# One pair of 1 MB input loads cut into rows and columns, in a gated recurrence with a slot mixture behind it

## The chip, the cores and the metric

The kernel runs on one core of a Trainium2 chip. The metric is the device time of one execution in microseconds (us), as the median of several runs; before the change it is 196.58 us (three runs, 196.49 to 196.69).

## What is computed

Two layers in a row. The first is a gated linear recurrence over 5056 tokens, for 4 batches and 256 channels; the second treats all 20224 tokens as one set and mixes them through 8 experts with 4 slots each.

```
# x, f_logit: (4, 5056, 256); lower_bound: (256,)
f = lower_bound + (1 - lower_bound) * sigmoid(f_logit)
for t in range(S):
    h = f[:, t] * h + (1 - f[:, t]) * x[:, t];  y[:, t] = h
# y as (20224, 256); phi: (256, 32); w1: (8, 256, 1024); w2: (8, 1024, 256)
logits = y @ phi
d = softmax of logits over the tokens;  slot_input = d.T @ y        # 32 slots
slot_out[e] = relu(slot_input[e] @ w1[e]) @ w2[e]                    # 8 experts, 4 slots each
c = softmax of logits over the slots;   out = c @ slot_out
```

The slots need all tokens, so the kernel has two parts with the experts between them: first everything is read, scanned and summed into slots; then the experts run on the 32 slots; then the 20 MB of output are computed and stored.

## The kernel before, in words

**Units.** The tokens of a batch are cut into 10 groups of 512 (the ninth has 448 new ones, the last is laid from the end). A unit is one group of one batch; there are `n_unit` = 40 of them, numbered from 0. Each unit passes through stages on different engines: its `f_logit` and `x` are loaded (`load`), ScalarE takes the sigmoid (`gate`, L235), GpSimd forms the product with `x` (`enter`, L246), TensorE turns both to channels (L250, L258, L265), ScalarE forms the decays (L298, L305), VectorE scans (L320, L333), TensorE turns the result back to tokens (L346) and sums it into the slots. The order of all instructions is written out by hand: one loop over the units, in which the engines get the steps of different units.

**Loads.** All inputs are loaded by SyncE in `load(n)`, called for every second unit, six units ahead of the scan (`AHEAD = 6`), `f_logit` first and `x` behind it. I write f(n) and x(n) for the two. Each fills one tile of two units, `f_t` or `x_t`; there are three buffers of each, so f(30) goes where f(24) was and can't start before the sigmoid of that tile is done, and x(30) where x(24) was, which GpSimd must have read. For units 0 to 3 and for the last four, each unit has loads of its own of 512 KB (L225). For units 4 to 31 (`long(n)`) a load is one DMA of 1 MB (L215): 1024 consecutive tokens, eight to a partition, so that each of the 128 partitions gets one run of 8 KB. Units 32 to 35, of the ninth group, use another split of 896 KB (L219). f(30) and x(30), called in unit 24, are the last pair of the long form; f(32), x(32), f(34), x(34) and the 512 KB loads of units 36 to 39 follow.

**Weights.** `w1` and `w2` (16 MB in 32-bit floats, 16 transfers of one expert's half, the last in two parts) are loaded by GpSimd (L137, L147), which writes them as 16-bit floats: four of them between the inputs, the others from unit 31 on, behind the inputs. The last two go into a tile of `f_t` (in the profile: `w_t`).

**Behind the loop.** The experts run as matmuls with `w1` (L653) and `w2` (L689, L703); `so_ps` is their sum, L715 scales it to `slot_out`, and from it the outputs are computed (L734, L813 and the scalings) and stored by SyncE in pieces of up to 4 MB.

**Names.** `P` = 128 partitions, `B` = 4 batches, `R` = 4 tokens per partition and unit, `D` = 256 channels, `G` = 512.

Of the kernel before, what the change touches and what calls it, by code (L numbers as in the profile page):

```python
# [18 lines left out]
def kernel(  # L19
# [10 lines left out]
    nc = tc.nc  # L30
    B, S, D = x.shape
# [4 lines left out]
    P = 128  # L36
    DC = D // P
    FC = F // P
    R = 4
    G = P * R  # L40
    n_grp = (S + G - 1) // G
    n_unit = n_grp * B
# [3 lines left out]
    def first(g):  # L46
        return g * G if g < n_grp - 1 else S - G

    def used(g):
        return first(g + 1) - first(g) if g < n_grp - 1 else G  # L50
# [116 lines left out]
    with tc.tile_pool(name="sp2", bufs=3) as sp2, \  # L167
# [23 lines left out]
        def long(n):  # L191
            return B <= n and by_pairs(n)

        def place(n):
            if by_pairs(n):
                t, j = divmod(n, 2 * B)
                return 2 * t + j % 2, j // 2
            return divmod(n, B)
# [4 lines left out]
        def tokens(src, n, k):  # L203
            g, b = place(n)
            v = src[ds(b, k), ds(first(g), G)]
            return v.rearrange("b (p r) d -> p b r d", r=R)

        def load(n, k=2):
            for src, dst, tag in ((f_logit, fs, "f_t"), (x, xs, "x_t")):
                if n % 2 == 0:  # L210
                    dst[n // 2] = ld.tile([P, 2, R, D], F32, name=tag, tag=tag)
                t = dst[n // 2]
                if long(n):
                    g, b = place(n)
                    nc.sync.dma_start(  # L215
                        out=t.rearrange("p u r d -> p (u r) d"),
                        in_=src[b, ds(first(g), 2 * G)].rearrange("(p r) d -> p r d", r=2 * R))
                elif n // B == odd:
                    nc.sync.dma_start(  # L219
                        out=t.rearrange("p u r d -> p (u r d)")[:, ds(0, R7 * D)],  # L220
                        in_=src[ds(n % B, 2), ds(first(odd), used(odd))].rearrange(
                            "b (p r) d -> p b (r d)", r=R7))
                else:
                    for m in range(n, n + k):
                        nc.sync.dma_start(out=t[:, ds(m % 2, 1)], in_=tokens(src, m, 1))  # L225
# [256 lines left out]
        for n in range(SINGLE):  # L482
            load(n, 1)
        load(SINGLE)
        lb_constants()
        gate(0, 1)
# [13 lines left out]
        for n in range(n_unit):  # L500
            if n < SINGLE - 2:
# [10 lines left out]
                if n % 2 == 0:  # L512
                    unit(load, n + AHEAD)
# [6 lines left out]
            else:  # L520
# [55 lines left out]
                elif not end and by_pairs(n - 1):  # L576
                    if n % B == 0:
                        g = (n - 1) // (2 * B) * 2
# [50 lines left out]
    with tc.tile_pool(name="ew", bufs=1) as ew, \  # L629
# [34 lines left out]
        for q in range(E // Q):  # L664
# [4 lines left out]
            if q == 0:  # L669
                nc.tensor.matmul(cs_ps, rep2, cs1, start=True, stop=True)  # L670
                src = ht_ps.rearrange("p f (j s) -> p f j s", s=NS)[:, :, :, ds(0, SPE)]
                src = bass.AP(tensor=src.tensor, offset=src.offset,
                              ap=[list(src.ap[0]), [P, FC], [NS + SPE, Q], [1, SPE]])
# [6 lines left out]
            for j in range(Q):  # L680
                s0 = (Q + j) * SPE
                src = ht_ps[:, :, ds(j * NS + s0, SPE)]
# [202 lines left out]
```

## Time and profile before

| | |
|---|---|
| median of three runs | 196.58 us (196.49 to 196.69) |
| the profiled execution | 196.66 us |
| its span, first to last instruction | 194.9 us |
| busy: TensorE, VectorE, ScalarE, GpSimd | 148.1, 141.8, 138.7, 102.5 us |
| read from HBM, written to it | 58.23 MB, 20.71 MB |
| SyncE's queue, share of the 16 DMA engines' span | 76.5% |
| GpSimd's queue | 21.6% |
| f(n) and x(n) of 1 MB, issue to landing, median | 12.2 and 11.0 us |

The page of the profile shows one execution. Its slices cut the span into 40 equal parts and give each engine's busy share in tenths; DMA is the mean share of the 16 DMA engines, GB/s what arrived (a weight counts half, as it is written in 16 bits). In a table by stretches, each engine has its busy microseconds and its instruction count, then come the granted clock of TensorE, the DMA share (it can pass 1, as packets of two queues overlap) and GB/s. The chain that ended last is given as start, length and what ran. A list of issues gives start, length, engine, line and tile; SPq is the queue of SyncE. A line of waits gives who waited for whom, the microseconds in total, how often, and the longest. A load that is issued waits in its queue behind others, so its 11 to 12 us to landing are mostly waiting.

### The profile page before, as it was taken

How to read it: one execution, taken by the hardware profiler on the slowest of the kernel's cores; microseconds unless marked ns; L12 is line 12 of the kernel's file. 1: busy time of each engine (PE TensorE's matmuls, PEld its weight loads, DVE VectorE, ACT ScalarE, POOL GpSimd, SP SyncE). 2: the span in 40 equal slices, each digit the busy share in tenths (PEclk: the TensorE clock that was granted, in tenths of full speed). 3: DMA queues.
4: the chain of work that ended last, by engine and by line, in shares of the span. 5: the costliest groups of instructions: out<-in, count | busy, mean ns of one | idle time of the engine just before them, and what ended most of it. 6: DMA issues, size and time to landing. Idle time of an engine off the chain costs nothing.

```text
span 194.9 us, 3264 instructions
## 1 busy us (share of the span) xinstructions
PE 148.1 (76%) x1215; PEld 106.6 (55%) x1216; DVE 141.8 (73%) x175; ACT 138.7 (71%) x193; POOL 102.5 (53%) x77
## 2 busy tenths in 40 slices
PE   0685887997999979899798976999695999970000
PEld 0464666685776757767585865667462763420000
DVE  2666799899799999999999999543178858860000
ACT  3686898799889999899988698531068789990000
POOL 2586778864998689874979978570030000000000
PEclk9998799699999999999999999999999555555555
DMA  6999999999999999999999999999839999999995
GB/s 203 415 431 427 427 429 425 425 422 375 363 425 429 406 330 427 420 432 350 380 416 410 255 219 213 215 214 213 168 142 432 424 454 431 431 431 430 431 431 222
DMA packets 11953, 70.75 MB, mean 363 GB/s; under 512 B 1297, under 2 KB 1682, under 8 KB 7458
## 3 DMA queue, kind: packets, MB, share of 16 engines
q1 hardware_dynamic: 9456, 62.13, 76.5%
q0 software_dynamic: 2480, 8.42, 21.6%
q8 instruction: 9, 0.15, 0.3%
q14 instruction: 6, 0.05, 0.1%
q10 hardware_dynamic: 2, 0.00, 0.0%
HBM read 58.23 MB, written 20.71 MB: 405 GB/s over the span
## 4 chain that ended last, share of the span: by engine, by line
PE 27%; DVE 23%; DMA 22%; ACT 12%; issue 3%; POOL 2%; SPq 1%; ACTq 0%; DVEq 0%; POOLq 0%
DVE h L333 14%; DMA w_t<-in_moe_w_dram 10%; PE op L813 7%; PE sp L250 5%; DMA w_sb<-in_moe_w_dram 5%; PE hp L346 5%; PE up L265 4%; DVE ht L365 4%; DMA f_t<-in_f_logit_dram 4%; DMA out_dram<-ob 3%; DVE h L320 3%; ACT s_t L235 3%; ACT oc L780 2%; ACT a L298 2%; POOL u_t L246 2%
## 5 line engine op out<-in xcount | busy, mean ns | idle before, releaser
L246 POOL TENSOR_TENSOR u_t<-s_t,x_t 128x1024 bf16<-128x1024 bf16 (+1 forms) x39 | 82.3, 2127 | 22.3 <-ACT s_t L235 14.0
L333 DVE TENSOR_TENSOR_SCAN h<-a,h,up 128x512 bf16<-128x512 f32 x64 | 78.1, 1268 | 6.6 <-PE up L265 2.7
L235 ACT ACTIVATE s_t<-f_t 128x2048 bf16<-128x2048 f32 (+2 forms) x23 | 38.2, 1668 | 5.1 <-DMA f_t<-in_f_logit_dram 5.0
L346 PE MATMUL hp<-ident_f,h 128*128 128x128 f32 (+1 forms) x160 | 29.1, 306 | 8.1 <-DVE ht L365 5.9
L346 PEld LDWEIGHTS hp<-ident_f,h 128*128 128x128 f32 (+1 forms) x160 | 23.4, 207 | 17.1 <-DVE ht L365 10.6
L298 ACT ACTIVATE a<-sp,lbs 128x1024 f32<-128x1024 bf16 x28 | 29.7, 1113 | 2.8 <-PE sp L250 2.7
L250 PE MATMUL sp<-ident_f,s_t 128*128 128x128 f32 x144 | 22.1, 299 | 7.3 <-ACT s_t L235 5.9
L265 PE MATMUL up<-ident_f,u_t 64*128 64x64 f32 x224 | 21.2, 233 | 2.4 <-POOL u_t L246 2.2
L250 PEld LDWEIGHTS sp<-ident_f,s_t 128*128 128x128 f32 x144 | 18.0, 154 | 9.1 <-ACT s_t L235 6.9
L728 ACT ACTIVATE ob<-op,rrow 128x256 f32<-128x256 f32 x32 | 12.3, 481 | 11.8 <-PE op L734 10.8
L265 PEld LDWEIGHTS up<-ident_f,u_t 64*128 64x128 f32 x224 | 16.7, 141 | 7.1 <-POOL u_t L246 2.9
L365 ACT COPY ht<-hp 128x512 f32<-128x512 f32 (+1 forms) x21 | 12.2, 581 | 5.3 <-PE hp L346 5.2
L305 ACT ACTIVATE a<-sp,lbs 128x512 f32<-128x512 bf16 (+2 forms) x16 | 13.2, 868 | 2.9 <-PE sp L250 2.6
L184 PE MATMUL slot_ps<-rep,ident_f 128*128 128x256 f32 x42 | 14.3, 431 | 0.0
L365 DVE COPY ht<-hp 128x512 f32<-128x512 f32 (+1 forms) x19 | 12.7, 669 | 0.9 <-PE hp L346 0.9
L813 PE MATMUL op<-slot_bd,etall 64*128 64x512 bf16 x32 | 13.1, 625 | 0.1
L824 ACT ACTIVATE oc<-op,rrow 128x256 f32<-128x256 f32 x32 | 12.2, 486 | 0.7 <-PE op L813 0.2
L734 PE MATMUL op<-slot_out,etall 32*128 32x256 bf16 x64 | 12.1, 363 | 0.1
L818 DVE TENSOR_TENSOR oc<-op,rrow 128x1024 f32<-128x1024 f32 x8 | 9.7, 1223 | 2.7 <-PE op L813 2.7
L724 DVE TENSOR_TENSOR ob<-op,rrow 128x1024 f32<-128x1024 f32 (+2 forms) x12 | 9.7, 862 | 2.6 <-DMA out_dram<-ob 2.0
L734 PEld LDWEIGHTS <-etall 32*128 32x128 bf16 x64 | 8.6, 152 | 3.6 <-issue 1.1
L379 PE MATMUL lg<-h,phi 128*32 128x512 bf16 (+1 forms) x80 | 10.5, 405 | 0.2 <-ACT et L403 0.2
(109 smaller groups left out, 166.9 us busy)
## 6 DMA issues: line engine op xcount, KB each, us to landing
f_t<-in_f_logit_dram SPq DMA_DIRECT2D x14, 1024.0 KB, 12.2
x_t<-in_x_dram SPq DMA_DIRECT2D x14, 1024.0 KB, 11.0
w_sb<-in_moe_w_dram POOLq DMA_DIRECT2D x14, 512.0 KB, 10.3
out_dram<-ob SPq DMA_DIRECT2D x3, 2048.0 KB, 10.5
f_t<-in_f_logit_dram SPq DMA_DIRECT2D x8, 512.0 KB, 8.6
x_t<-in_x_dram SPq DMA_DIRECT2D x8, 512.0 KB, 7.7
out_dram<-oc SPq DMA_DIRECT2D x1, 4096.0 KB, 14.6
out_dram<-oc SPq DMA_DIRECT2D x2, 2048.0 KB, 15.9
```

The source lines that it names most:

```text
L184: nc.tensor.matmul(slot_bank[:, 1], ident_f, wide_rep, start=first, stop=False, skip_group_check=True)
L235: nc.scalar.activation(s_t, f_t, ACT.Sigmoid, scale=-1.0)
L246: nc.gpsimd.tensor_tensor(uts[n][:, :r], s_t[:, :r], x_t[:, :r], ALU.mult)
L250: nc.tensor.transpose(ps[:, :, r], t[:, r].bitcast(F32), ident_f)
L265: nc.tensor.transpose(v[:, :, r], t(r)[k].bitcast(F32), ident_f[k, k])
L298: nc.scalar.activation(a, sp[:, :, :, :, o], ACT.Identity, scale=nomlb[:, ds(o, 1)], bias=1.0)
L305: nc.scalar.activation(decays[n // 2, o][:, ds(n % 2, k), :T], sp[:, ds(n % 2, k), :T, o], ACT.Identity, scale=nomlb[:, ds(o, 1)], bias=1.0)
L333: nc.vector.tensor_tensor_scan(h[:, :T, o], decays[n // 2, o][:, n % 2, :T], up[:, :T, o], hs[number(g - 1, b)][:, ds(used(g - 1) - 1, 1), ...
L346: nc.tensor.transpose(hp[:n_p, r], hw[:, :n_p, r], ident_f)
L365: copy(hts[g][:n_p, b].rearrange("p r d -> p (r d)").bitcast(F32), hps.pop(n)[:n_p].rearrange("p r c -> p (r c)"))
L734: nc.tensor.matmul(op[:, j], ew[:, :, r + j], slot_out[ds(b * NS, NS)], start=True, stop=True, skip_group_check=True)
L813: nc.tensor.matmul(op[:, i_r].rearrange("p u d -> p (u d)"), ew[:, :, r + i_r], slot_bd[ds(j * 2 * NS, 2 * NS)].rearrange("s u d -> s (u d)"),
```

## The change

`load` gets a list of parts for the long form. For every long load the tile and the source are now addressed with eight tokens of a partition as one run; with a single part (all 128 rows, all columns) this is one DMA as before. For unit `LEAN` = 40 - 8 - 2 = 30, x(30) becomes three DMAs: 112 rows, 8 rows, 8 rows. f(30) becomes seven: 112 rows, 8 rows, 8 rows without their last 1 KB, and that last 1 KB of these eight rows in DMAs of 4, 2, 1 and 1 rows. The bytes are the same, and so is the place where each goes; SyncE issues eight DMAs more.

```
+        LEAN = n_unit - 2 * B - 2
+        ALL = 2 * R * D
+        LEAN_F = ((0, 112, 0, ALL), (112, 8, 0, ALL), (120, 8, 0, ALL - D),
+                  (120, 4, ALL - D, D), (124, 2, ALL - D, D),
+                  (126, 1, ALL - D, D), (127, 1, ALL - D, D))
+        LEAN_X = ((0, 112, 0, ALL), (112, 8, 0, ALL), (120, 8, 0, ALL))
...
                 if long(n):
                     g, b = place(n)
-                    nc.sync.dma_start(
-                        out=t.rearrange("p u r d -> p (u r) d"),
-                        in_=src[b, ds(first(g), 2 * G)].rearrange("(p r) d -> p r d", r=2 * R))
+                    to = t.rearrange("p u r d -> p (u r d)")
+                    at = src[b, ds(first(g), 2 * G)].rearrange("(p r) d -> p (r d)", r=2 * R)
+                    parts = ((0, P, 0, 2 * R * D),)
+                    if n == LEAN and tag == "f_t":
+                        parts = LEAN_F
+                    if n == LEAN and tag == "x_t":
+                        parts = LEAN_X
+                    for p, k_p, c, k_c in parts:
+                        nc.sync.dma_start(out=to[ds(p, k_p), ds(c, k_c)],
+                                          in_=at[ds(p, k_p), ds(c, k_c)])
```

## The prediction

> **What bounds the kernel now.** I read the page's slices first, then the engines by stretches of time, the chain that ended last, SyncE's issues and the waits.
>
> ```profile
> DMA  6999999999999999999999999999839999999995
> ```
> ```profile
> 84.00:88.00 4.00, 3.82 (x30) 2.58 (x27) 4.00 (x4) 3.95 (x6) 3.98 (x3) 1.00 1.02 429
> 120.00:130.00 10.00, 9.80 (x159) 7.18 (x160) 5.28 (x9) 5.26 (x11) 7.15 (x9) 1.00 1.06 214
> 130.00:139.00 9.00, 7.61 (x102) 5.80 (x95) 3.46 (x9) 1.40 (x4) 0.51 (x2) 1.00 1.06 212
> 139.00:142.00 3.00, 2.11 (x16) 1.64 (x17) 0.01 (x1) 0.00 (x0) 0.00 (x0) 1.00 0.52 92
> ```
> Next to last is the DMA share. All 16 DMA engines work without a gap from 3 to 139 us, through the inputs and the weights behind them; only from 139 to 142 us do some run out before others.
>
> ```profile
> 111.56 10.21 DMA w_sb<-in_moe_w_dram
> 121.77 0.28 issue
> 122.06 18.78 DMA w_t<-in_moe_w_dram
> 140.83 0.04 issue
> 140.87 1.09 PE so_ps L703 x8
> 141.96 0.02 issue
> 141.99 0.50 DVE slot_out L715
> ```
> The chain ends its first part on the last weights; everything later (stores until 194 us) starts from them. So a microsecond on the DMA engine that finishes last at 141.5 us is a microsecond of the kernel, and work on an engine that finishes early is free. The DMA engines differ. The completion marks of a transfer's sixteen shares, as offsets from the first, are in the trace:
>
> ```
> x(30), first mark 86.64: 0 .02 .03 .09 .10 .13 .20 .21 .33 .52 .54 .83 1.53 1.60 1.61 1.65
> last w, first mark 139.77: 0 .09 .10 .30 .54 .55 .64 1.13 1.17 1.38 1.55 1.63 1.66 1.68 1.71 1.75
> ```
> Every engine moves 8 KB in 0.309 us (packets 0.306 apart), so the lag comes from elsewhere: instruction packets of 16 KB at 29.6, 47.3, 62.5, 77.0, 92.6, 105.0, 124.0 and 134.9 us. Each puts another engine some 1.24 us back (before 29.6 the largest offset is 0.42, after it one stands at 1.66); the 8 KB ones (44.8, 57.4, 64.8, 100.0, 135.3) cost about 0.5. The first packets of the kernel start in two groups of eight, 1.74 to 1.82 and 2.00 to 2.11 us. Following packets end to start, the first two hits fall in the second group. By the offsets that vanish at each hit I put the first seven there and the eighth (134.9) and the 8 KB ones in the first group. At the end, then, six of the second group stand at 1.55 to 1.75, and the first group at 0 to 0.64 with two at about 1.15 and 1.38.
>
> **The change part by part.** It concerns f(30) and x(30).
>
> ```profile
> 73.36 0.33 SPq L215 DMA_DIRECT2D x_t<-in_x_dram  x1
> 73.78 0.38 SPq L215 DMA_DIRECT2D f_t<-in_f_logit_dram  x1
> 78.00 0.33 SPq L215 DMA_DIRECT2D x_t<-in_x_dram  x1
> 78.42 0.66 SPq L219 DMA_DIRECT2D f_t<-in_f_logit_dram  x1
> 82.93 0.56 SPq L219 DMA_DIRECT2D x_t<-in_x_dram  x1
> 83.58 0.56 SPq L219 DMA_DIRECT2D f_t<-in_f_logit_dram  x1
> 88.78 0.54 SPq L219 DMA_DIRECT2D x_t<-in_x_dram  x1
> ```
> They are x(28), f(30), x(30), f(32), x(32), f(34), x(34).
>
> The other long loads only get another view. Their trace rows already are 128 runs of 8,192 bytes, so I cost that at nothing; were it not merged, rows of 1 KB (46 ns each) would add an eighth to every load.
>
> Bytes: each engine's share of 8 rows becomes 7; 16 rows per tensor move into narrow DMAs. The one narrow DMA of the trace, the single row of the lower bound, has its packet at 1.61 to 1.81 us, and a first-group engine starts its first row at 1.814; so I put the narrow ones on the first group. The second group then saves 2 x 0.306 = 0.61 us. The first adds 4 pieces less 2 rows: +0.57 us (the 7 KB piece at 0.27), and on one engine four 1 KB packets at 0.043 and six more completions, +0.8. In the opposite case, all on the second group, its six late engines go up by 0.6.
> The Trainium skill (DMA: Bandwidth & Descriptors, section "Why a DMA increments its semaphore by 16 and not by 1") says that a DMA from SyncE uses the largest count up to 16 that divides its rows, on the lowest-numbered engines. By that rule 112 rows use all sixteen and 8 rows the first eight, and the sum stays at the +0.57 and -0.61 above; no run here shows an 8-row load yet.
>
> SyncE: eight more issues at 0.33 to 0.5, 2.6 to 4 us. Those of f fit into the gap of 73.78 to 78.00. But SyncE's DMAs take eight semaphores in turn, and a DMA waits until the one eight before it has landed: x(4) issued at 5.66 us, x(0) landed at 5.64. GpSimd's weights do the same:
>
> ```profile
> POOL w_t L147 <- DMA w_sb<-in_moe_w_dram: 2.8, 2, 2.0
> ```
> Now eight before is eight before in ten small ones. The fifth, sixth and seventh f pieces wait for f(26), x(26), f(28) (76.0, 78.5, 80.9). The 112 rows of x wait for x(28), landed at 83.38, instead of going at 78.00. The next piece of x waits for the 112 rows of f, which the late engines finish one row sooner than the 85.86 of now: 85.55. The last x piece follows at 85.97, f(32) at 86.36 instead of 78.42, with x(32) and f(34) queued behind it; the first packet comes 1.0 us after an issue (0.72 to 1.74 at the start): 87.4. x(32) at 87.1 and f(34) at 87.7 are early enough, x(34) keeps 88.78, and from there the queue is as deep as before.
>
> What starves: x(28) ends on the early engines at 81.62; f(30) with its pieces runs to 84.4, x(30)'s first packet comes at 84.4: nothing lost. The 112 rows end at 86.5; the next pieces come at 86.55 and 86.95, to 87.2; f(32) at 87.4 to 87.6. Now f(32) starts on the early engines at 86.5, on unhit ones of the second group at 86.6 to 86.8, on the four late ones at 88.1. So the first group shifts by +0.9 (0.6 work, the rest idle), the unhit second group by +0.8 (all idle), the late four by -0.5. The start of f(32) lines all engines up, and hits after it fall on engines that have lost their lead.
>
> Sum at the last weights: second-group engines hit at 92.6 and 105.0: 1.6 + 0.8 = 2.4. First-group engine hit at 134.9: 1.38 + 0.9 = 2.3. The late four: 1.7 - 0.5 = 1.2. The largest goes from 1.75 to 2.4, **+0.6 us**, all of it on the path. Compute hides nothing and loses nothing: x(30) lands by 87.7 (88.29 now), f(32) by about 90 (91.09 now). Bounds: a first packet 0.85 us after the issue (143.60 to 144.45, a store) makes it +0.45; 1.3 us, as for a second issue of 0.66 in the way, +0.9. The profiled execution took 196.66 us, its span 194.9 and 1.8 around it; the median, 196.58, is 0.08 below. 196.58 + 0.6 = 197.2 us, own range 196.9 to 197.6.
>
> **Rivals.** No stall: if the framework lets the pieces pass without those waits, only bytes move. The second group falls to 1.14, the first rises to 1.38 + 0.7 = 2.1: +0.3, 196.9 us. Against it stand the two waits above.
>
> Faster: the rows leave the late engines as the diff arranges it, no wait bites, and the instruction packets of 134.9 and 135.3 us fall on engines that were made lighter (they follow the instruction streams, whose timing can move). Then the first group's largest is 0.84 + 0.65 = 1.5 and the second's 1.14 plus little: 1.75 to about 1.4, 196.2 us. It decides only if both conditions hold; for it speaks that six of the eight relieved engines are the latest ones.
>
> Narrow rows collide: the eight rows of a piece lie in neighbouring partitions, and if four of them must pass one at a time, a piece takes 4 x 0.309 instead of 0.309. Four pieces add 3.6 us to the first group: 1.38 + 0.6 + 3.6 = 5.6, +3.9, 200.5 us; two at a time, +1.2 on it and about 198.1. Nothing in the trace writes so few partitions from several engines; the loads at L219, split in other shapes, run at full rate (7 KB in 0.272), which speaks weakly against it.
> The Trainium skill (SBUF — State Buffer, section "Door 1: The DMA port swizzle") says that bandwidth depends on how many of 16 ports the partitions reach, four neighbours sharing one; by it rows 112 to 119 have two ports, which is the one-at-a-time case.
>
> That the change does nothing would need no landing to matter; the saturated DMA rules it out, short of terms that cancel.
>
> **How the numbers follow.** Forecast 0.45, no stall 0.15, collision 0.25, faster 0.15. 0.2%, about what a measurement of this kernel can tell from no change, is 0.39 us. Slower by more: 0.38 of the forecast, the collision, 0.05 of the second, 0.68. Within: 0.07, 0.10 and 0.05, 0.22. Faster: 0.10. The range reaches from 196.2 to 200.0, leaving out the top of the collision and the best of the faster case.
>
> **What would show it.** Right: the 112 rows of x issued near 83.4, the next x piece near 85.5 and f(32) near 86.4; a DMA share below 1 between 84 and 88; the last weights landing near 142.1. Wrong: issues of x at 78 (no stall); row packets of 0.6 us or more in the narrow pieces (collision); the last landing before 141.4 (faster).

## The result, and the profile after

The changed kernel takes 203.99 us (203.75 to 204.53, four runs); the one before took 196.6 us on the same chip. The ratio is 1.038 [1.037, 1.039]: 7.4 us slower, where +0.6 was forecast and 200.0 was the top of the range. Some executions of a kernel take one to two per cent longer than the rest (205.35 us beside 201.98 to 203.39 in one kernel below); ratios leave them out. The profiled execution took 204.19 us, its span 202.4.

The DMA share of the 40 slices, and the rates under it:

```profile
DMA  4999999999999999999999999999909999999995
GB/s 203 418 430 424 431 423 429 424 427 318 423 427 423 351 390 427 257 253 259 425 417 415 280 206 215 189 211 213 173 6 405 425 433 440 418 431 447 418 431 246
```

In the DMA row there is no dip where one was forecast, between 84 and 88 us: it reads 9 throughout. The rate below it does fall: three slices of 5 us, from 81 to 96 us, move 257, 253 and 259 GB/s where their neighbours move 425 to 427. The engines are busy, but slow. The same in steps of 2 us, for the kernel after and then for the kernel before (busy time and count of PE, PEld, DVE, ACT, POOL; then granted clock, DMA share, GB/s):

```profile
82.00:84.00 2.00, 2.00 (x22) 1.49 (x22) 2.00 (x3) 2.00 (x3) 1.01 (x1) 1.00 1.11 258
84.00:86.00 2.00, 2.00 (x19) 1.38 (x14) 2.00 (x3) 1.98 (x3) 0.85 (x1) 1.00 0.73 184
86.00:88.00 2.00, 1.82 (x14) 1.42 (x13) 2.00 (x3) 1.96 (x3) 1.98 (x3) 1.00 1.03 279
88.00:90.00 2.00, 1.90 (x22) 1.50 (x21) 2.00 (x3) 0.50 (x1) 1.99 (x1) 1.00 1.00 248
92.00:94.00 2.00, 0.87 (x5) 0.56 (x4) 1.38 (x3) 2.00 (x3) 0.00 (x0) 1.00 1.17 237
```

```profile
82.00:84.00 2.00, 2.00 (x22) 1.71 (x22) 2.00 (x3) 2.00 (x3) 1.01 (x2) 1.00 1.04 438
84.00:86.00 2.00, 2.00 (x19) 1.23 (x16) 2.00 (x2) 1.98 (x3) 2.00 (x1) 1.00 0.98 414
```

Two things are in these lines. From 84 to 86 us the DMA share falls to 0.73: that is the stall of the forecast, 0.5 us per engine. In the other lines of the kernel after, the share is full and the rate is 237 to 279 GB/s, some six tenths of the 414 to 438 of before. When the first engines leave x(28) and start the 112 rows of f(30), packets of 8 KB become slow: from 82 to 90 us they take 0.43 to 0.60 us in the mean of each microsecond; before, all of them took 0.309. The packets of x(28) that are still running on the later engines slow down with them, and x(28) lands at 84.99 instead of 83.38. No narrow piece takes part yet: the 112 rows of f(30) get their sixteen completion marks from 85.56 to 88.35, and the first mark of an 8-row piece comes at 86.12.

SyncE's issues, which answer to those of before:

```profile
73.36 0.33 SPq L230 DMA_DIRECT2D x_t<-in_x_dram  x1
73.78 7.52 SPq L230 DMA_DIRECT2D f_t<-in_f_logit_dram  x7
85.05 4.06 SPq L230 DMA_DIRECT2D x_t<-in_x_dram  x3
89.32 0.66 SPq L233 DMA_DIRECT2D f_t<-in_f_logit_dram  x1
90.11 0.55 SPq L233 DMA_DIRECT2D x_t<-in_x_dram  x1
```

The waits are the predicted ones: f(30)'s seven parts are issued over 7.5 us, the last three behind the landings of f(26), x(26) and f(28); x(30) waits for x(28), its second part for f(30)'s 112 rows (landed 88.35, issue 88.37), and f(32) goes at 89.32 instead of 78.42. The waits of SyncE at this line over the whole kernel (who for whom, microseconds, times, longest) hold them; before, they were 2.2 us in 2 waits and 0.5 us in 1:

```profile
SPq L230 <- DMA f_t<-in_f_logit_dram: 8.4, 6, 3.0
SPq L230 <- DMA x_t<-in_x_dram: 6.6, 3, 3.7
```

Behind the loads compute now starves. The first line has the waits of GpSimd's product for `x`, the longest, 6.1 us, for x(30); the next two are from the timelines of ScalarE and TensorE; the last two show the clock in 40 slices, before and after:

```profile
POOL u_t L260 <- DMA x_t<-in_x_dram: 11.3, 7, 6.1
```
```profile
98.17 1.70 ACT L249 ACTIVATE s_t<-f_t 128x1792 bf16<-128x1792 f32 x1 [3.45 <-DMA f_t<-in_f_logit_dram]
```
```profile
100.39 0.75 PE L360 MATMUL hp<-ident_f,h 128*128 128x128 f32 x4 [2.44 <-ACT ht L379]
```
```profile
PEclk9998799699999999999999999999999555555555
PEclk9998799999999999999955559999999755555555
```

x(30) lands at 95.9 us (88.29 before) and f(32) at 98.1 (91.09 before), the sigmoid waits 3.45 us for f(32), TensorE has a hole of 2.4 us, and from 101.1 us its granted clock is at half for 20.5 us; before, it stood at full from 38.9 to 151.5 us. The stretches at the end, and the end of the chain:

```profile
130.00:139.00 9.00, 8.80 (x141) 6.76 (x139) 5.10 (x8) 4.68 (x10) 7.81 (x11) 1.00 1.05 199
139.00:142.00 3.00, 2.89 (x46) 1.75 (x43) 1.55 (x3) 1.49 (x4) 0.00 (x0) 1.00 1.06 213
142.00:149.00 7.00, 7.00 (x92) 5.71 (x91) 2.10 (x6) 0.53 (x2) 0.00 (x0) 1.00 0.63 119
```
```profile
138.92 1.89 PE hi_ps L667 x32
...
146.89 0.87 PE tail L156 x2
147.76 1.76 PE so_ps L717 x16
149.53 0.02 issue
149.55 0.50 DVE slot_out L729
```

The last weights land 5.8 us later (their 384 KB part at 146.62 instead of 140.83), and the DMA share is full until then. But the end no longer waits for them. TensorE, which before was busy for 2.11 of the 3 us from 139 to 142 and waited for weights in the rest, now works without a gap from 142 to 149, and `slot_out` starts 7.6 us late. So there are two losses in a row: 5.8 us on the DMA engines, and some 1.8 us of TensorE that has fallen behind the weights.

### The profile page after: what moved, and what is told of

Read it like the earlier page. It is cut to its first block, busy times and chain, and to the rows that moved or that the text cites. A ratio compares the mean times of both kernels' runs of the same rounds, so it can differ in the third digit from the quotient of the medians.

```text
span 202.4 us, 3276 instructions
## 1 busy us (share of the span) xinstructions
PE 155.3 (77%) x1216; PEld 111.9 (55%) x1216; DVE 142.5 (70%) x175; ACT 138.6 (68%) x193; POOL 102.5 (51%) x77
## 4 chain that ended last, share of the span: by engine, by line
PE 40%; ACT 19%; DMA 15%; POOL 5%; issue 5%; DVE 4%; SPq 1%; ACTq 0%; POOLq 0%
DMA f_t<-in_f_logit_dram 15%; PE op L827 6%; PE hp L360 6%; ACT s_t L249 5%; PE op L748 5%; POOL u_t L260 5%; PE sp L264 5%; DVE h L347 3%; PE slot_ps L184 3%; ACT a L319 2%; PE up L279 2%; ACT oc L794 2%; ACT a L312 2%; PE lg L393 2%; PE so_ps L717 2%
## 5 line engine op out<-in xcount | busy, mean ns | idle before, releaser
L360 PE MATMUL hp<-ident_f,h 128*128 128x128 f32 (+1 forms) x160 | 31.3, 324 | 9.8 <-ACT ht L379 5.0
L360 PEld LDWEIGHTS hp<-ident_f,h 128*128 128x128 f32 (+1 forms) x160 | 25.0, 210 | 19.0 <-DVE ht L379 8.3
L279 PE MATMUL up<-ident_f,u_t 64*128 64x64 f32 x224 | 22.0, 238 | 2.7 <-POOL u_t L260 2.6
L279 PEld LDWEIGHTS up<-ident_f,u_t 64*128 64x128 f32 x224 | 17.3, 145 | 7.6 <-POOL u_t L260 3.4
L184 PE MATMUL slot_ps<-rep,ident_f 128*128 128x256 f32 x42 | 16.4, 485 | 0.0
L334 DVE TENSOR_TENSOR_SCAN h<-a,h,up 128x224 bf16<-128x224 f32 x16 | 9.6, 663 | 4.2 <-PE up L272 4.2
```

Of the source, the lines that this page charges most:

```text
L184: nc.tensor.matmul(slot_bank[:, 1], ident_f, wide_rep, start=first, stop=False, skip_group_check=True)
L279: nc.tensor.transpose(v[:, :, r], t(r)[k].bitcast(F32), ident_f[k, k])
L360: nc.tensor.transpose(hp[:n_p, r], hw[:, :n_p, r], ident_f)
```

## The experiments

Two sums are taken from each trace. The DMA work per engine is the time of all packets that start between 60 us and "last w", over 16; "last w" is the landing of the 384 KB part, and "late" is against its 140.83 us before. The idle time per engine counts how many of the 16 engines have no packet, from 60 us to 2 us before last w; behind that the engines run out one after another. Before, they are 83.38 and 0. Where exactly the window ends moves the work by some 0.2 us.

**The clock.** The kernel after, with idle matmuls of TensorE (a filler that the kernel has already) put into the units where the hole opens:

```
+            idle({28: 5, 29: 2, 30: 2}.get(n, 0))
             unit(scan, n)
```

> The changed kernel with nine more idle matmuls (0.43 us each at full clock) in units 28, 29 and 30, written into a bank region that nothing reads, where TensorE stood idle from 97.9 to 100.4 us. Theory 'clock' (the late x(30) and f(32) leave a hole on TensorE, the granted clock drops to 0.5 for 20.5 us from 101.1 us, and the slower matmuls make most of the 7.4 us): no half-clock stretch between 95 and 125 us, and 198 to 200 us, so 4 to 6 us of the 7.4 come back. Rival 'late data' (the lost time is the late landing of x(30) and f(32) itself, +7 us on f(32), and the clock only follows): 203 to 205 us whatever the clock shows, since the matmuls fill time that was idle or add up to 2 us.

202.26 us, 1.028 [1.026, 1.030]. Neither theory has it: the first expected 198 to 200 us, the second 203 to 205. The clock stays full from 51.8 to 154.2 us, the last w is where it was (146.69, 5.86 late), and the chain ends on weights again:

```profile
146.69 0.04 issue
146.73 1.07 PE so_ps L718 x8
147.80 0.02 issue
147.83 0.49 DVE slot_out L730
```

So the clock is worth some 1.7 us of the 7.4 (203.99 - 202.26), and the rest, 5.7, is about the lateness of the weights.

**The same DMAs with all rows.** f(30) in seven and x(30) in three column parts, each of all 128 rows: as many DMAs, issues and waits, no narrow rows.

```
LEAN_F = ((0, P, 0, 1280),) + tuple((0, P, 1280 + 128 * i, 128) for i in range(6))
LEAN_X = ((0, P, 0, 1792), (0, P, 1792, 128), (0, P, 1920, 128))
```

> f(30) again in seven DMAs and x(30) in three, so the same number of issues, the same turn of the eight semaphores and the same waits of SyncE, but each DMA has all 128 rows and takes a part of the columns (f: 5 KB and six of 512 B; x: 7 KB and two of 512 B). Theory 'waits' (the ten small DMAs hold SyncE until x(28) and the first f piece have landed, so f(32) is issued near 86 instead of 78 us and w_sb gets ahead of it): x's first part issued near 83.4, f(32) near 86 to 87, and most of the loss stays, 200 to 204 us. Theory 'slow packets' (the 112-row and 8-row DMAs run at 258 GB/s instead of 425, and this makes the waits long enough to hurt): 8 KB-equivalent rates stay full, DMA share dips little, and the time is 196.6 to 197.8 us.

198.68 us, 1.010 [1.009, 1.012], between the ranges of the two theories. Here the forecast's timetable comes true: the first part of x(30) is issued at 83.71 (83.4 forecast), the next at 85.26 (85.5), f(32) at 86.16 (86.4), with 0.45 us of idle engines. Packets of 8 KB keep their time (0.309), and those of 5 KB take 0.196. The last w is 2.22 late: 0.45 idle, and 1.42 more work (some 0.5 from 1024 packets of 512 bytes, 0.027 us each where a sixteenth of an 8 KB packet is 0.019; 0.6 from packets of 7 KB, single ones of which take 0.6 to 1.02 us right beside the idle time and up to 1.07 at 87.8 us). The rest is the end: in the last 2 us before last w an engine has nothing for 0.90 us in the mean, where it was 0.36 before. The waits with their idle time thus cost at most some 2 us, not 7.4.

**Fewer DMAs, few rows.** Two parts of 112 and 16 rows for both tensors; and f(30) in two halves of 64 rows with x(30) in 96 and 32:

```
e3: LEAN_F = LEAN_X = ((0, 112, 0, ALL), (112, 16, 0, ALL))
e4: LEAN_F = ((0, 64, 0, ALL), (64, 64, 0, ALL))
    LEAN_X = ((0, 96, 0, ALL), (96, 32, 0, ALL))
```

> f(30) and x(30) in two DMAs each, 112 rows and 16 rows: the 112-row DMA of the change without its narrow pieces and without long waits on the semaphores (two DMAs more instead of eight, x issued near 78, f(32) near 79). Theory 'slow packets': the packets of the 112-row parts take about 0.48 us on the mean instead of 0.309, the 16-row parts as long or longer, each tensor takes some 1.5 to 2 us more on the DMA engines, and the time is 198 to 201 us, or more if TensorE's clock drops. Theory 'waits': SyncE does not stall, so at most +0.5 us, 196.6 to 197.2.

> A look at packet times by number of rows: f(30) in 64 and 64 rows, x(30) in 96 and 32 rows, all 8 KB per row, two DMAs each. If the slowness comes from where the rows of one engine lie (a DMA of fewer than 128 rows gives each engine consecutive rows, and two or more engines then meet on the same part of the memory), packets of the 64-row parts take about 0.6 us (two by two), of the 96-row part between 0.31 and 0.6, of the 32-row part 0.6 to 1.2. If it is the row count 112 itself or the narrow pieces beside it, all packets take 0.309. Time 197 to 202 us by the first, 196.6 to 197.1 by the second.

112 + 16: 1.030 [1.028, 1.032], that is 202.42 and 202.86 us, above the 198 to 201 of its first theory (which allowed for more). Its trace is of a longer execution, 206.97 us, and isn't used. 64 + 64 and 96 + 32: 206.49 us in a single execution, above the 197 to 202 expected, also without a long wait. Its last w is 8.72 late, with 7.60 more work; packets of 8 KB took 0.82 to 0.91 us from 82 to 84 us, where the first 64 rows of f(30) run beside x(28), and 0.56 to 0.70 from 84 to 90. Neither part of f(30) is narrow here, and two DMAs are enough, so the cost comes from the rows. The rates of this kernel:

```profile
82.00:84.00 2.00, 1.83 (x16) 1.67 (x17) 2.00 (x3) 1.53 (x3) 1.28 (x1) 1.00 1.11 168
84.00:86.00 2.00, 2.00 (x19) 1.16 (x17) 2.00 (x3) 2.00 (x2) 0.00 (x0) 1.00 0.91 188
```

**A cut by columns first.** All rows without their last 1 KB, then that 1 KB for 120 rows and for 8 rows:

```
LEAN_F = LEAN_X = ((0, P, 0, ALL - D), (0, 120, ALL - D, D), (120, 8, ALL - D, D))
```

> The same shift of bytes between DMA engines as the change, made another way: f(30) and x(30) each in three DMAs, all 128 rows of 7 KB, then the last 1 KB of 120 rows and of 8 rows. Four DMAs more instead of eight, so SyncE is not held long. If only rows in 112s and 8s are slow and eight engines take the narrow parts, all packets of 7 KB stay at 0.272 us, half of the engines carry 16 KB less, the other half 16 KB more, and the lag of the last weights decides: theory 'slow packets' 196.3 to 197.3 us. By the first prediction's tally of lags (engines of the first group at 1.38 us rise by 0.6) +0.2 to +0.3 us, 196.9; if the relieved engines are the last ones, -0.3, 196.3. If any narrow part is dear, 198 us or more.

198.02 us, 1.007 [1.006, 1.009]; 1.17 late, with 1.16 more work and no idle. So the last case of the expectation holds: this cut is dear as well. But it isn't the change's shift of bytes, as the expectation took it to be. The part of 120 rows lands with 15 completion marks and the part of 8 rows with 8, so one engine gets nothing of the 120 rows and the others their usual share, where the change takes a row of 8 KB from each of eight engines. The work comes mostly from the packets of 7 KB, which take 0.30 to 0.34 us from 84 to 89 us while the narrow parts run, and 0.272 before.

**The stall taken away, and each half alone.** Three parts for both tensors (112, 8, 8), so that no part waits long; f(30) as in the change with x(30) whole; x(30) as in the change with f(30) whole:

```
e6: LEAN_F = ((0, 112, 0, ALL), (112, 8, 0, ALL), (120, 8, 0, ALL))
e7: LEAN_X = ((0, P, 0, ALL),)
e8: LEAN_F = ((0, P, 0, ALL),)
```

> The change without the column pieces: f(30) and x(30) both in 112, 8 and 8 rows, four DMAs more instead of eight. Seven column and narrow issues less stand ahead of x(30), and its 112 rows wait for x(24) instead of x(28), so they are issued near 78 and f(32) near 81. Theory 'slow packets, and the stall adds about 1 us': the last weights land 5 to 6 us later than before, 202 to 203.5 us. Theory 'the stall starts it' (idle DMA engines at 85 to 87 us and w_sb ahead of f(32) are the cause): 197 to 199 us.

> f(30) in its seven parts, x(30) whole. One 112-row DMA instead of two. Theory 'slow packets': the added DMA time scales with the number of 112-row DMAs and of what is in flight beside them, about half of the 5.4 us per engine, 199 to 201 us. SyncE is held for x(28) alone (x(30) issued near 84 or 85), and f(32) follows at once near 85.5, so the stall costs up to 1 us of this.

> x(30) in 112, 8 and 8 rows, f(30) whole. One 112-row DMA and two DMAs more, no wait worth naming. Theory 'slow packets': about half of the 5.4 us per DMA engine, 198.5 to 200.5 us; packets of 8 KB between 0.45 and 0.6 us while the 112 rows are in flight, on engines that still carry f(30) too. Theory 'stall': no change, 196.6 to 197.

| | ratio | last w late | more work | idle | clock at half after 60 us (before the end) |
|---|---|---|---|---|---|
| after | 1.038 [1.037, 1.039] | 5.79 | 5.28 | 0.51 | 20.5 us |
| no stall (112, 8, 8) | 1.037 [1.034, 1.039] | 6.75 | 6.70 | 0 | 6.8 us |
| f(30) alone | 1.020 [1.017, 1.023] | 3.12 | 2.46 | 0.56 | none |
| x(30) alone | 1.020 [1.018, 1.022] | 4.33 | 4.30 | 0 | 3.4 us |
| 64 + 64, 96 + 32 | one execution | 8.72 | 7.60 | 0.28 | 20.5 us |

f(30) alone falls into its expected range; no stall and x(30) alone lie 0.1 and 0.2 us above theirs. Without the stall f(32) is issued at 80.80, no engine idles, and nothing is gained: the time is the same within the interval. Work replaces the idle time, since the slow rows of f(30) and x(30) now run beside each other and beside f(32). With the parts of the change, more work and idle time together give the lateness to 0.1 us; with 64 rows 0.84 is missing, and the engines' end has it: in the last 2 us before last w they have nothing for 1.25 us in the mean (0.36 before).

**Which rows go together.** In the last four kernels x(30) is whole and f(30) is cut in other ways, each with at most five parts: even rows and odd rows; 4 DMAs of 8 neighbouring rows and one of 96; 4 DMAs of 8 rows, every fourth one of the first 32, and the same 96; 4 DMAs of 32 rows, every fourth one. With a start, a number and a step:

```
e9:  64 rows from 0 and from 1, step 2
e10: 8 rows from 0, 8, 16 and 24, step 1; 96 rows from 32, step 1
e11: 8 rows from 0, 1, 2 and 3, step 4;   96 rows from 32, step 1
e12: 32 rows from 0, 1, 2 and 3, step 4
```

> f(30) as two DMAs of 64 rows, the even ones and then the odd ones; x(30) is one DMA. Theory (rows of neighbouring partitions share a way into the memory, so it matters which rows are written at the same time): 64 rows taken from all over the 128 partitions reach every way, where the halves of the run with 64 + 64 rows reached one half of them and had packets of 0.61 us. Mean of the 8 KB packets from 82 to 90 us below 0.40 us, last w within 1 us of before (140.8 to 141.8). Rival (a DMA of fewer than 128 rows is slow, whichever rows these are): packets of 0.6 us again from f(30), last w 2.5 to 4 us late.

> f(30) as four DMAs of 8 neighbouring rows (0 to 31) and one of the other 96; x(30) is one DMA. Five parts, so no part has to wait long for its semaphore. Theory (neighbouring partitions share a way): the 32 packets of the four pieces take 0.6 to 1.2 us instead of 0.309, and eight engines get 1.2 to 3.6 us of extra work from them, beside what the 96 rows cost. Rival (fewer than 128 rows are slow as such): about 0.5 us, as the 112 rows, and the same as in the run with every fourth row.

> The same as the run with four DMAs of 8 neighbouring rows, but each piece takes every fourth row of the 32 (0, 4 to 28; then 1, 5 to 29 and so on). The same DMAs, sizes, issues and waits; only which rows go together differs. Theory (neighbouring partitions share a way): the packets of the four pieces take 0.31 to 0.35 us, and the last w comes 1 us or more before that of the run with neighbouring rows. Rival (fewer than 128 rows are slow as such): no difference between the two, within 0.3 us.

> f(30) as four DMAs of 32 rows, every fourth one; x(30) is one DMA. Theory (neighbouring partitions share a way): all ways are reached by every DMA, packets from 82 to 90 us below 0.40 us in the mean and the last w within 1 us of before. Rival (fewer than 128 rows are slow as such, or what counts is the fixed share of rows that each engine gets): 0.5 us and more, the last w 2.5 us late or more.

A single execution of each, beside 196.78 us for the kernel before:

| | us | last w late | more work | mean of the 8 KB packets, 80 to 100 us |
|---|---|---|---|---|
| 64 rows, step 2 | 197.39 | 0.39 | 0.29 | 0.311 us |
| 8 neighbours, 96 rows | 202.05 | 5.22 | 4.35 | 0.494 us |
| 8 rows of step 4, 96 rows | 201.18 | 4.33 | 3.66 | 0.461 us |
| 32 rows, step 4 | 196.90 | 0.01 | 0.06 | 0.309 us |

The second line of the 64 + 64 kernel above has 188 GB/s; here are the same two stretches with even and odd rows, and then with 32 rows of step 4:

```profile
82.00:84.00 2.00, 1.55 (x13) 1.39 (x13) 2.00 (x3) 1.82 (x2) 1.55 (x1) 1.00 1.02 430
84.00:86.00 2.00, 2.00 (x20) 1.24 (x20) 2.00 (x3) 1.85 (x2) 1.31 (x1) 1.00 1.00 422
```
```profile
82.00:84.00 2.00, 2.00 (x21) 1.38 (x21) 2.00 (x3) 2.00 (x3) 1.37 (x2) 1.00 1.02 426
84.00:86.00 2.00, 2.00 (x18) 1.43 (x14) 2.00 (x3) 1.98 (x3) 2.00 (x2) 1.00 1.01 426
```

The two kernels with evenly taken rows meet the theory's expectation. A DMA of 64 or of 32 rows is not slow: taken evenly over the partitions it runs at full rate, and four DMAs in the place of one cost nothing that a single execution can show. 64 rows from one half of the partitions took 1.8 to 2.9 times as long a packet (that kernel cuts x(30) too, but from 82 to 84 us only f(30)'s first half and x(28) run, at 0.82 to 0.91). So the rival (fewer than 128 rows are slow as such) falls. By the Trainium skill (SBUF — State Buffer, section "Door 1: The DMA port swizzle") 64 neighbouring partitions reach only 8 of 16 ports, while every second or every fourth partition reaches all of them; the 0.56 to 0.91 us against 0.309 agree with it. The 112 rows of the change and the 96 of these kernels reach all the ports by that table and are slow nevertheless, so the number of ports alone doesn't decide. What else does stays open: no run here shows which row went to which engine. Nor do the runs part the two ends of a load: a row is always the same 8 KB of HBM too, so rows that are neighbours where they are written are neighbours where they are read.

The kernel with 8 rows of step 4 missed its expectation, and with it the simple form of the theory. An 8-row piece lands with eight completion marks, one of each engine that it runs on, so the distance between the marks of one piece and the next is the time of a packet. With every fourth row it is 0.57, 0.60 and 0.61 us in the mean, where 0.31 to 0.35 was expected; with neighbouring rows it is 0.64, 0.63 and 0.62, where 0.6 to 1.2 was expected. Only the first piece comes clearly earlier (mean mark 83.11 instead of 83.76), and the last w 0.89 us, short of the 1 us expected; executions of one kernel differ by as much (f(30) alone: 199.50 to 201.26 us). The 96 neighbouring rows run in both kernels, behind the pieces on eight engines and beside them on the other eight. So the runs show that parts which each take rows evenly from all 128 partitions keep the full rate, and that a part of 64, 96 or 112 neighbouring rows is slow and makes slow what runs beside it; they don't show that the rows of one small piece decide.

No version tried is faster than the kernel before.

## Why the prediction was wrong, step by step

- **The bound.** Right. The DMA engines carry the kernel to the last weights, and in most runs their added work and idle time are the lateness: 5.28 + 0.51 for 5.79 us after, 6.70 for 6.75, 2.46 + 0.56 for 3.12, 4.30 for 4.33.
- **The other view of the long loads.** Right: cost nothing. With 32 rows of step 4 the kernel has it too, and its last w is 0.01 us from that of before. (The alternative was priced low: eight rows of 1 KB at 46 ns are 0.37 us, a fifth above 0.309 and not an eighth. Nothing hung on it.)
- **The bytes, the step that failed.** "Each engine's share of 8 rows becomes 7" took the 112 rows at 7 x 0.306. The count is right: 112 rows land with 16 completion marks and 8 rows with 8, so the rule of the Trainium skill that is cited there agrees with the trace. The time is not: the 112 rows, and what ran beside them, took 0.43 to 0.60 us a packet. Up to 100 us that is 3.2 us per engine in packets of 8 KB and 1.0 in those of 7 KB (0.322 in the mean instead of 0.275), most of the 5.3 us of added work. The 0.61 us that each late engine was to save is small beside it. Why neighbouring rows are slow is the part of the cause that stays open.
- **The collision rival.** Right in kind, wrong in its place, size and chance. It priced the 8-row pieces and left the 112 rows alone; the 112 rows were slow from 82 us on, before the first 8-row piece, and the run with 112 + 16 rows shows +5.9 us without any. Its 0.25 came from the row held against it, the loads at L219 at full rate "in other shapes". These too write all 128 partitions, and so they said nothing of fewer rows. The rule of the Trainium skill beside it points to neighbouring rows, but by its count of ports the 112 rows would have been fine.
- **The semaphore waits.** Right in mechanism and order; with full-rate packets (the column parts) the issues up to f(34) come within about 0.3 us of the forecast. In the changed kernel those from x(30) to f(34) are 1.7 to 3.1 us late, since x(28) and the 112 rows land late.
- **The idle time.** The forecast's split (0.3 us on eight engines, 0.8 on four, little on four) is some 0.35 us in the mean; measured 0.51, and it buys nothing to remove it. In the column parts, with the idle time but without the slow rows, the last w is 2.2 us late instead of 0.6: some 0.5 of it belongs to the packets of 512 bytes that this variant adds, and 0.6 to slow single packets, first ones beside the idle time, which the forecast lacked.
- **The tally of lags by engine** (1.75 to 2.4 us). Not tested: the traces name no engine for a packet, and the instruction packets on which it counts moved (105.0, 124.0 and 134.9 us became 108.9, 134.9 and 144.2).
- **"Compute hides nothing and loses nothing."** It failed with the size: x(30) and f(32) land 7 us late or more, TensorE runs dry, and the half clock costs some 1.7 us behind the weights.
- **The signs it named.** "Row packets of 0.6 us or more in the narrow pieces" looked at the wrong pieces: the eight packets of the 7 KB one took 0.276 to 0.462, slow too, but under the sign. "A DMA share below 1 between 84 and 88" was seen, 0.73 and 0.88 over the whole; it was the smaller part.

## What to carry to other kernels

Before a load is cut by rows, ask which rows each part takes together: 64 rows taken as every second one ran at the full rate, and 64 neighbouring rows took 1.8 to 2.9 times as long a packet. A row of the trace excludes a cost only if it shares the property in question; loads in another shape but with all 128 rows were no witness for 112. And a DMA share of 1 says that the engines are busy, not that they are fast: read the GB/s beside it.

## What the runs showed of the hardware

- A DMA of 112 neighbouring rows slows what runs beside it: x(28), a whole load, landed 1.6 us late with f(30)'s rows behind it (0.1 us late where f(30) was whole), and the 128-row loads of 7 KB took 0.339 us a packet beside x(30) alone in its parts, 0.275 before.
- SyncE's DMA of 128, 112, 96, 64 or 32 rows lands with 16 completion marks, one of 120 rows with 15, and ones of 8, 4, 2 and 1 rows with 8, 4, 2 and 1.
- First packets after a time in which engines had nothing are slow: seven eighths of a row in 0.6 to 1.02 us in the column parts (0.272 later), and at the start of the kernel before 4 KB in 0.61 to 0.87 us (0.16 in the mean after 60 us).
- On TensorE a hole of 2.4 us, in a stretch of 8 us (92 to 100) that had 4.1 us of work, was followed by 20.5 us at half the clock. The lateness of the weights alone doesn't set this: without the stall they were later still, and it was 6.8 us.
